# Sketch attention feeding an ELU MLP: the first two query groups computed from squares of sketch sums and differences

## The chip, the core and the metric

The kernel runs on one core of a Trainium2 chip. The metric is the device time of one execution in microseconds (us). The core has five engines with queues of their own: TensorE (PE in the profile; its weight loads are PEld), VectorE (DVE), ScalarE (ACT), GpSimd (POOL) and SyncE (SP, which only issues DMAs here). Each queue runs in program order; engines wait for one another through semaphores.

## The reference

```python
def phi(x):
    a = np.einsum('rd,bhsd->bhsr', S1, x)
    b = np.einsum('rd,bhsd->bhsr', S2, x)
    return np.einsum('bhsi,bhsj->bhsij', a, b).reshape(*x.shape[:-1], r * r)
q_p, k_p = (phi(q), phi(k))
kv = np.einsum('bhsf,bhsd->bhfd', k_p, v)
z = np.sum(k_p, axis=2)
num = np.einsum('bhsf,bhfd->bhsd', q_p, kv)
den = np.einsum('bhsf,bhf->bhs', q_p, z)[..., None] + 1e-06
attn = num / den
...
h = x @ w_in                                    # x: attn as (tokens, heads * 32)
g = np.where(h > 0.0, h, np.exp(np.minimum(h, 0.0)) - 1.0)
out = g @ w_out
```

There are 4 batches, 4 heads, 1088 positions, head size 32 and r = 8 sketches, so 64 features; 4352 tokens of 128 channels enter the MLP, whose hidden size is 2048. Everything is computed in float32. S1, S2, w_in and w_out arrive as float64 and are rounded to float32 on the chip.

## The kernel before, in words

The 4352 tokens are cut into groups of 512 (8 half tiles of 64 positions; the last group is smaller). Groups 0 and 1 belong to batch 0. For each group the attention part makes xg[g], a 128x512 tile with channels on partitions. The MLP then goes through 8 pairs of hidden chunks: mm1(g, cp) multiplies with w_in (L840, through the helper `quarters`, L253 to L257, which splits the 128 output columns into tiles of width[0] = 32), elu_a makes a relu and an exp on ScalarE (L861, L863), elu_d combines them on VectorE into gg (L869), and mm2 or its variants multiply with w_out. `steps` (L1004) gives the order of the pairs; mm2 runs two steps behind mm1. Everything is emitted by hand in the order that the queues are to have (`manual_schedule`), and the `extra` table hangs the attention work of later groups onto steps.

Rounding a weight chunk i is a chain: RA (VectorE, L102), RB (ScalarE, L107), then RS, RM, RD, RE on VectorE (L117, L121, L129, L137). Chunk 0 is w_in of pair 0, chunk 1 w_in of pair 1, chunk 2 w_out of pair 0, chunk 3 w_out of pair 1. RC_2 does RS, RM and RD of chunks 0 and 1 in one 512-wide instruction each.

Before the first mm1 the kernel must get batch 0's kv and z and the query features of group 0. The order, L946 to L1000:

- keep_warm (L260) issues matmuls of constants whose result nobody reads. L300 and L287 turn the sketch matrices into the tiles Sab, SXh and SW; `transp` (L280) turns k and q on VectorE.
- KF (L343) makes the key sketches, copied by ScalarE (L351). z_tile (L424), Z (L256) and Z_out (L465) make z. KO_pool (GpSimd, L322, tiles 0 to 3) and KO_first (VectorE, L416, tiles 4 to 8) make the 64 key features; KA (L435) sums kv over the positions. KS_first copies kv twice side by side (L481), turns it (L482) and stores it as kvS (L483).
- Group 0: q1_first (L505) makes the query sketches, copied by L509; q1z_first (L517) makes their products with z. q2_den multiplies and sums to den (L588, L593), takes the reciprocal (L594) and scales one sketch by it (L596); q2_out forms the 64 features per token and head as an outer product on VectorE (L609, two parts). q4_early turns them (L621, eight 128x128 turns on TensorE, each four copied by L622); q5_early multiplies with kvS (L628) and ScalarE copies the result to xg (L634).
- Group 1 goes the same way through q1_second (L526, L530), q2 and q4_early, interleaved with mm1_first and the first ELUs of group 0.

mm1_first (L847) is mm1 of group 0 and pair 0 in two column halves, outer loop over the halves. PSUM has eight banks, handed out by tag: "h" four in rotation, "aux" two, "o0" and "o1" one each. mm1 of a step writes to the "h" banks that the step two before used.

Of the kernel before, what the change touches and what calls it, by code (L numbers as in the profile page):

```python
# [27 lines left out]
def kernel(  # L28
# [21 lines left out]
    nc = tc.nc  # L50
# [45 lines left out]
    nc.gpsimd.memset(tiny[:], 2.0 ** -20)  # L96

# [206 lines left out]
    nc.gpsimd.tensor_copy(SW[:, :, :2, :].rearrange("p h x r -> p h (x r)"), Sab[:])  # L304

# [27 lines left out]
    kv_ps, feats, wzs, kf_ps = {}, {}, {}, []  # L333
# [106 lines left out]

    def KT_out(b):

        kt = work.tile([P, 2 * D], F32, name="kvt", tag="kvt")
        nc.vector.transpose(kt[:], kv_ps[b][:, :R * R])
        nc.sync.dma_start(kvd[b], kt[:])
        src = kvd[b].rearrange("(h p) x -> p h x", h=H)
        for w in range(4 if b in kvs else 0):
            nc.sync.dma_start(kvs[b][32 * w:32 * w + 32].rearrange("p h f d -> p h (f d)"), src)
        for u in (0, 1) if b in pair_b else (b // 2,):
            for f in range(2):  # L450
                r = slice(64 * u + 32 * f, 64 * u + 32 * f + 32)
                nc.sync.dma_start(kv2[b][r], src[:, :, D * f:D * f + D])
# [20 lines left out]
    def Z_first():  # L473
# [3 lines left out]
        return ps, ZC(0, ps)  # L477

    def KS_first():
        kd = work.tile([P, 2, R * R], F32, name="kd", tag="kd", bufs=1)  # L480
        nc.scalar.copy(kd[:], _ap(kv_ps[0][:, :R * R], [[0, 2], [1, R * R]]))  # L481
        nc.tensor.transpose(kv_ps[0][:, 128:256], kd[:].rearrange("p w f -> p (w f)"), ident[:])  # L482
        nc.scalar.copy(kvS[:].rearrange("p h d -> p (h d)"), kv_ps[0][:, 128:256])  # L483
# [16 lines left out]
    def q1_first():  # L500
        p = psum.tile([P, 512], F32, name="abqp", tag="aux")
        for i in range(4):
            for u in range(2):
                b, t = half_tile(0, 2 * i + u)
                nc.tensor.matmul(p[64 * u:64 * u + 64, i * 64:i * 64 + 64], qT[b][:, t, :],  # L505
                                 Sab[:].rearrange("p h y -> p (h y)"),
                                 skip_group_check=True, tile_position=(0, 64 * u))
        abw[0] = work.tile([P, H * 4, 2 * R], F32, name="abq", tag="abq", bufs=1)
        nc.scalar.copy(abw[0][:].rearrange("p (h t) y -> p h t y", h=H),  # L509
                       p[:, :256].rearrange("p (t h y) -> p h t y", t=4, h=H))  # L510

    def q1z_first():
        p = psum.tile([P, 512], F32, name="zqp", tag="h", bufs=4)
        for i in range(4):
            for u in range(2):
                b, t = half_tile(0, 2 * i + u)
                nc.tensor.matmul(p[64 * u:64 * u + 64, i * 32:i * 32 + 32].rearrange("p (h r) -> p h r", h=H),  # L517
                                 qT[b][:, t, :], SW[:, :, 2, :], skip_group_check=True, tile_position=(0, 64 * u))
        return p[:, :128].rearrange("p (t h r) -> p h t r", t=4, h=H)

    def q1_second():
        p = psum.tile([P, 512], F32, name="abwp", tag="h", bufs=4)
        for i in range(4):
            for u in range(2):
                b, t = half_tile(1, 2 * i + u)
                nc.tensor.matmul(p[64 * u:64 * u + 64, i * 96:i * 96 + 96], qT[b][:, t, :],  # L526
                                 SW[:].rearrange("p h x r -> p (h x r)"), skip_group_check=True,
                                 tile_position=(0, 64 * u))
        abw[1] = work.tile([P, H * 4, 3 * R], F32, name="abw1", tag="abq1", bufs=1)
        nc.scalar.copy(abw[1][:].rearrange("p (h t) y -> p h t y", h=H),  # L530
                       p[:, :384].rearrange("p (t h y) -> p h t y", t=4, h=H))


# [43 lines left out]
    def q2(g, parts=1, between=None):  # L577
        q2_den(g, None, between)
        q2_out(g, parts)

# [17 lines left out]

    def q2_out(g, parts=1, between=None):
        m = H * qn[g]  # L600
        x, an = abw.pop(g), ans.pop(g)
        qp[g] = work.tile([P, 4 * H, R, R], F32, name="qp", tag="qp", bufs=2)
        for i in range(parts):
            if i and between:
                between()
            h = slice(i * m // parts, (i + 1) * m // parts)
            a_ = an[:, h]
            b_ = x[:, h, :R]
            nc.vector.tensor_mul(qp[g][:, h], _ap(a_, list(a_.ap[1:]) + [[0, R]]),  # L609
                                 _ap(b_, [b_.ap[1], [0, R], b_.ap[2]]))  # L610

    def q4_early(g):

        qpT[g] = work.tile([P, H, 2, P], F32, name="qpT", tag="qpT", bufs=2)
        for hh in range(2):
            p = psum.tile([P, 512], F32, name="qtp", tag="aux")
            for h2 in range(2):
                for m in range(2):
                    o = (h2 * 2 + m) * P
                    r = (2 * hh + h2) * 4 + 2 * m  # L620
                    nc.tensor.transpose(p[:, o:o + P], qp[g][:, r:r + 2].rearrange("p t i j -> p (t i j)"), ident[:])  # L621
            nc.scalar.copy(qpT[g][:, 2 * hh:2 * hh + 2], p[:].rearrange("p (h m s) -> p h m s", h=2, m=2))  # L622

    def q5_early(g):
        xp = [psum.tile([P, 512], F32, name="xps", tag="aux") for _ in range(2)]
        for h in range(H):
            for w in range(2):
                nc.tensor.matmul(xp[w][D * h:D * h + D, :256], kvS[64 * w:64 * w + 64, h, :],  # L628
                                 qpT[g][64 * w:64 * w + 64, h].rearrange("p m s -> p (m s)"),
                                 skip_group_check=True, tile_position=(64 * w, D * h))  # L630
        xg[g] = work.tile([P, 512], F32, name="xg", tag="xg", bufs=3)
        to = xg[g][:].rearrange("p (m w s) -> p w m s", w=2, s=P)
        for w in range(2):
            nc.scalar.copy(to[:, w], xp[w][:, :256].rearrange("p (m s) -> p m s", s=P))  # L634

# [211 lines left out]
    def mm1_first():  # L847
        hs[0, 0] = [psum.tile([P, 512], F32, name="h", tag="h", bufs=4) for c in range(2)]
        for w in range(2):
            for c in range(2):  # L850
                cols = [x[:].rearrange("p (m w s) -> p w m s", w=2, s=P)[:, w] for x in (hs[0, 0][c], xg[0])]
                quarters(cols[0], W[:, 0, c * P:c * P + P], cols[1])
# [97 lines left out]
    zps, zl = Z_first()  # L950
    q1_first()
    KO_pool()
    KO_first(4, 5)
    KO_first(5, 7)
    Z(0, zps, zl)
    Z_out(0, zps)
    KO_first(7, KT)
    keep_warm(1, 96, 64)
    zq = q1z_first()
    q2_den(0, zq, lambda: RA(0))  # L960
    q2_out(0, 2, lambda: RA(1))
# [12 lines left out]
    keep_warm(1, 192, width[0])  # L974
    mm1_first()
    q2(1, 2, lambda: RA(2))
# [227 lines left out]
```

## Time and profile before

| what | value |
|---|---|
| median of 3 runs | 261.85 us (261.8 to 262.11) |
| the profiled execution's own time | 262.34 us |
| its span, first to last instruction | 260.6 us |
| mean granted TensorE clock | 0.998 |
| PE busy | 254.8 us (98%), 4123 matmuls |
| DVE busy | 186.9 us (72%), 352 instructions |
| ACT busy | 183.4 us (70%), 358 instructions |
| POOL busy | 159.0 us (61%) |

The span leaves out 1.74 us around the first and last instruction. Times in the trace count from the span's start. A line of the chain that ended last gives start, length, engine, the tile written, the source line and the number of instructions; a fp32 matmul call makes two TensorE instructions, a turn (transpose) makes one. A line of instruction groups gives line, engine, operation, output and input tiles, shape, count, then busy us and mean ns of one, then the idle time before them and what ended it. Busy shares are averages over stages with different limits; the stage in question here is the first 24 us.

### The profile page before, as it was taken

To read this page: it belongs to the slowest core of one execution; us is meant where nothing else is said; L and a number is where in the kernel's file an instruction comes from. 1 tells how busy PE (TensorE), PEld (TensorE's weight loads), DVE (VectorE), ACT (ScalarE), POOL (GpSimd) and SP (SyncE) were. 2 spreads that over 40 slices of the span, in tenths; PEclk is the share of its full clock that TensorE was granted. 3 is DMA by queue.
4 is the path that set the end of the run, shared out by engine and by line. 5 is a ranking of instruction groups with operands and counts; after the bars stand their busy time and mean duration, and the time that the engine had idled before them with its cause. 6 is when DMAs were issued, how large, how long until landed. Compare 5 with 4: busy or idle time off the path is not lost.

```text
span 260.6 us, 9756 instructions
## 1 busy us (share of the span) xinstructions
PE 254.8 (98%) x4123; PEld 158.4 (61%) x4123; DVE 186.9 (72%) x352; ACT 183.4 (70%) x358; POOL 159.0 (61%) x202
## 2 busy tenths in 40 slices
PE   8899999999999999999999999999999999999994
PEld 6753333453346667666666666665666666668993
DVE  6799999999988967997477675744466746544651
ACT  2379968766667577776687777775877777777792
POOL 3520007002179996788678798888688888887310
PEclk9999999999999999999999999999999999999999
DMA  5998079012112210002100204220001110110021
GB/s 173 330 358 222 3 223 268 24 21 85 28 18 28 31 34 18 3 15 34 20 0 4 33 10 104 60 30 13 3 3 27 34 26 3 25 19 3 3 30 33
DMA packets 30379, 15.61 MB, mean 60 GB/s; under 512 B 22496, under 2 KB 28000, under 8 KB 30336
## 3 DMA queue, kind: packets, MB, share of 16 engines
q1 hardware_dynamic: 29904, 14.63, 23.0%
q8 instruction: 32, 0.52, 0.9%
q10 hardware_dynamic: 368, 0.30, 0.3%
q0 software_dynamic: 64, 0.07, 0.1%
q14 instruction: 11, 0.09, 0.1%
HBM read 11.31 MB, written 2.36 MB: 52 GB/s over the span
## 4 chain that ended last, share of the span: by engine, by line
PE 97%; DVE 1%; ACT 0%; issue 0%; DVEq 0%
PE h L256 45%; PE pb L790 17%; PE pa L790 13%; PE o L256 5%; PE pb L766 4%; PE ol L256 3%; PE idle L264 1%; PE kv L435 1%; PE abp L343 1%; PE h L681 1%; PE h L551 1%; PE qtp L621 1%; DVE qp L609 1%; PE h L693 1%; PE xps L628 0%; PE kfps L365 0%
## 5 line engine op out<-in xcount | busy, mean ns | idle before, releaser
L256 PE MATMUL h<-xg,W 128*32 128x512 f32 (+3 forms) x904 | 130.8, 539 | 0.4 <-ACT xg L634 0.4
L869 DVE SCALAR_TENSOR_TENSOR gg<-e,h 128x512 f32<-128x512 f32 x128 | 85.9, 681 | 52.6 <-ACT e L863 47.8
L861 ACT ACTIVATE e<-h 128x512 f32<-128x512 f32 x128 | 75.5, 590 | 46.2 <-PE h L256 46.0
L863 ACT ACTIVATE e<-e 128x512 f32<-128x512 f32 x128 | 80.9, 632 | 3.8
L751 POOL TENSOR_TENSOR tt<-gg 128x512 f32<-128x512 f32 x50 | 64.3, 1286 | 28.9 <-DVE gg L869 25.2
L256 PEld LDWEIGHTS h<-xg,W 128*32 128x32 f32 (+1 forms) x904 | 43.0, 122 | 43.0 <-issue 34.4
L754 POOL TENSOR_TENSOR tt<-gg,tt 128x256 f32<-128x256 f32 x50 | 36.9, 739 | 3.9
L753 POOL TENSOR_TENSOR tt<-tt,gg 128x256 f32<-128x256 f32 x50 | 36.7, 734 | 3.9
L790 PEld LDWEIGHTS pa<-gg,W 128*64 128x64 f32 (+1 forms) x496 | 23.7, 126 | 22.4 <-issue 22.2
L790 PE MATMUL pa<-gg,W 128*64 128x128 f32 (+1 forms) x496 | 30.6, 274 | 0.0
L790 PE MATMUL pb<-tt,SS 128*64 128x128 f32 (+1 forms) x480 | 29.6, 273 | 0.0
L790 PEld LDWEIGHTS pb<-tt,SS 128*64 128x64 f32 (+1 forms) x480 | 22.8, 126 | 0.0
L790 PE MATMUL pa<-tt,SS 128*32 128x128 f32 (+1 forms) x288 | 21.2, 273 | 0.0
L790 PE MATMUL pb<-gg,SS 128*64 128x128 f32 (+1 forms) x256 | 19.9, 273 | 0.0
L790 PE MATMUL pb<-tt,W 128*64 128x128 f32 (+1 forms) x256 | 19.9, 273 | 0.0
L134 POOL TENSOR_TENSOR raw<-raw,tiny 128x512 f32<-128x512 f32 x1 | 1.0, 1041 | 24.7 <-DVE raw L129 24.7
L256 PE MATMUL o<-gg,W 128*32 128x512 f32 x128 | 15.3, 595 | 0.0
L790 PEld LDWEIGHTS pa<-tt,SS 128*32 128x32 f32 (+1 forms) x288 | 13.7, 124 | 0.0
L790 PEld LDWEIGHTS pb<-gg,SS 128*64 128x64 f32 (+1 forms) x256 | 12.8, 125 | 0.0
L790 PEld LDWEIGHTS pb<-tt,W 128*64 128x64 f32 (+1 forms) x256 | 12.8, 125 | 0.0
L766 PE MATMUL pb<-gg,W 128*32 128x256 f32 x192 | 11.5, 380 | 0.0
L921 DVE SCALAR_TENSOR_TENSOR gg<-e,h 128x256 f32<-128x256 f32 x16 | 6.6, 418 | 6.4 <-PE h L256 3.2
(163 smaller groups left out, 269.3 us busy)
## 6 DMA issues: line engine op xcount, KB each, us to landing
raw<-in_moe_w_in_dram SPq DMA_DIRECT2D x8, 256.0 KB, 6.3
raw<-in_moe_w_out_dram SPq DMA_DIRECT2D x8, 256.0 KB, 6.5
out_dram<-ob SPq DMA_DIRECT2D x112, 16.0 KB, 1.5
hd_k<-in_k_dram SPq DMA_DIRECT2D x3, 544.0 KB, 7.5
hd_q<-in_q_dram SPq DMA_DIRECT2D x3, 544.0 KB, 8.5
v<-in_v_dram SPq DMA_DIRECT2D x4, 288.0 KB, 7.1
v<-in_v_dram SPq DMA_DIRECT2D x4, 256.0 KB, 8.4
raw<-qpF SPq DMA_DIRECT2D x16, 64.0 KB, 2.0
```

The source lines that it names most:

```text
L256: nc.tensor.matmul(dst[c:c + tile], lhs[:, c:c + tile], rhs, skip_group_check=True, tile_position=(0, c), **kw)
L264: nc.tensor.matmul(idle[c:c + tile, :cols], ones[:, :tile], ones[:, :cols], skip_group_check=True, tile_position=(0, c))
L343: nc.tensor.matmul(ps[i // 5][64 * u:64 * u + 64, 64 * (i % 5):64 * (i % 5) + 64], kT[b][:, u * KT + i, :], Sab[:].rearrange("p h y -> p ( ...
L751: nc.gpsimd.tensor_tensor(_ap(t[:, 0], [[4 * P, 2], [P, 2], [1, P]]), _ap(gs[g, cp][:, 0, P:], [[4 * P, 2]] + us), _ap(gs[g, cp][:, 0], [[ ...
L753: nc.gpsimd.tensor_tensor(t[:, 1], t[:, 2], b11, op=ADD)
L754: nc.gpsimd.tensor_tensor(t[:, 3], b21, t[:, 1], op=SUB)
L766: nc.tensor.matmul(acc[1][0][r:r + width[0], 256 * hi:256 * hi + 256], lhs[:, w:w + width[0]], gg[:, c, 256 * u:256 * u + 256], start=(cp ...
L790: nc.tensor.matmul(bank[r:r + width[0], P * col:P * col + P], lhs[:, w:w + width[0]], rhs[:, u], start=(first and i in ((0,) if g == 1 els ...
L861: nc.scalar.activation(e, hs[g, cp][c][:, :n], RELU, scale=-1.0)
L863: nc.scalar.activation(e, e, EXP, scale=-1.0)
L869: nc.vector.scalar_tensor_tensor(gs[g, cp][:, c, :n], es[g, cp][:, c, :n], -1.0, hs[g, cp][c][:, :n], op0=ADD, op1=MAX)
L921: nc.vector.scalar_tensor_tensor(gs["last", k // 2][:, k % 2, :2 * P], es["last", k // 2][:, k % 2, :2 * P], -1.0, hs["last", k][:, :2 * P ...
```

## The change

Groups 0 and 1 no longer form the outer product of the two sketches a and b. Since a b = ((a + b)^2 - (a - b)^2) / 4, the change builds the 64 sums and 64 differences of sketch rows once (make_Spm) and lets one matmul per head (q_sums: 32 rows of one head, 128 output features, 512 tokens) produce all a + b and a - b with features on partitions. ScalarE squares them (q_squares, eight of 128x512). Because the features are already on partitions, no features are turned: x_sums multiplies the squares with kvS over all 128 rows, and KS_copy scales kvS's two halves by +0.25 and -0.25.

The division moves behind that sum. az makes, with 128 tokens as the stationary operand, one sketch and its product with z side by side; az_copy moves the first to SBUF, den_a and den_b make 1/den; den_wide (ScalarE) repeats each 1/den over its head's 32 channels; den_out turns that as four whole 128x128 blocks; den_copy brings it to SBUF; x_out multiplies it on VectorE with the x_sums result into xg.

In the order of the program, q_sums(0) stands where q1_first stood; the kv sum is split in two (KA_first: tiles 4 to 6 ahead of az(0), the rest after it); the second part of q is turned on VectorE before the first den; RC_2 is no longer used, chunks 0, 1 and 2 go through RS to RE one by one; the keep_warm calls behind the start are gone; mm1_first has the hidden chunk as its outer loop; width[0] is 64 from mm1_first to the first w_out, then 32 again. KT_out of batch 0 reads the SBUF copy kds of kv and no longer its PSUM bank.

```diff
+    quarters_pm = const.tile([P, 1], F32, name="qpm")
+    nc.gpsimd.memset(quarters_pm[:64], 0.25)
+    nc.gpsimd.memset(quarters_pm[64:], -0.25)
...
+    Sc = const.tile([FD, R], F32, name="Sc")
+    nc.scalar.copy(Sc[:], sps[:, :R])
...
+    Spm = const.tile([FD, 2, R, R], F32, name="Spm")
...
+    def make_Spm():
+        for s, op in enumerate((ADD, SUB)):
+            nc.vector.tensor_tensor(Spm[:, s], _ap(sps[:, R:], [[1, R], [0, R]]), _ap(Sc[:], [[0, R], [1, R]]), op=op)
...
+    def KA_first(tiles, first):
+        if first:
+            kv_ps[0] = psum.tile([P, 512], F32, name="kv", tag="o1", bufs=1)
+        for i in tiles:
+            for h in range(H):
+                nc.tensor.matmul(kv_ps[0][32 * h:32 * h + 32, :R * R], vt[0][:, (h * KT + i) * D:(h * KT + i + 1) * D],
+                                 feats[0, i // 5][:, i % 5, h].rearrange("p i j -> p (i j)"),
+                                 start=(first and i == tiles[0]), stop=(not first and i == tiles[-1]),
+                                 skip_group_check=True, tile_position=(0, 32 * h))
...
-        nc.vector.transpose(kt[:], kv_ps[b][:, :R * R])
+        nc.vector.transpose(kt[:], kv_ps[b][:, :R * R] if b else kds[0][:, 0])
...
-        return ps, ZC(0, ps)
-    def KS_first():
-        kd = work.tile([P, 2, R * R], F32, name="kd", tag="kd", bufs=1)
+        return ps
...
+    def KS_kd():
+        kd = kds[0] = work.tile([P, 2, R * R], F32, name="kd", tag="kd", bufs=1)
         nc.scalar.copy(kd[:], _ap(kv_ps[0][:, :R * R], [[0, 2], [1, R * R]]))
-        nc.tensor.transpose(kv_ps[0][:, 128:256], kd[:].rearrange("p w f -> p (w f)"), ident[:])
-        nc.scalar.copy(kvS[:].rearrange("p h d -> p (h d)"), kv_ps[0][:, 128:256])
+    def KS_turn():
+        nc.tensor.transpose(kv_ps[0][:, 128:256], kds[0][:].rearrange("p w f -> p (w f)"), ident[:])
...
+    def KS_copy():
+        nc.scalar.mul(kvS[:].rearrange("p h d -> p (h d)"), kv_ps[0][:, 128:256], quarters_pm[:])
...
-    def q1_first():
...
+    def tokens(g, rows, t0=0, t1=8):
+        b, t = half_tile(g, t0)
+        return qT[b][rows, t:t + t1 - t0, :].rearrange("p t s -> p (t s)")
...
+    def q_sums(g, half=None):
+        c = slice(0, 512) if half is None else slice(256 * half, 256 * half + 256)
+        for h in range(H):
+            if not half:
+                tag = "o0" if h == 3 else "h" if g or h == 2 else "aux"
+                sums[g, h] = psum.tile([P, 512], F32, name="qs", tag=tag, bufs={"o0": 1, "h": 4, "aux": 2}[tag])
+            rows = slice(32 * h, 32 * h + 32)
+            nc.tensor.matmul(sums[g, h][:, c], Spm[rows].rearrange("p s i j -> p (s i j)"),
+                             tokens(g, rows, c.start // 64, c.stop // 64), skip_group_check=True, tile_position=(32 * h, 0))
+
+    def q_squares(g, h):
+        if h % 2 == 0:
+            sq[g, h // 2] = work.tile([P, 2, 512], F32, name="sq", tag=("qp", "qpT")[g], bufs=2)
+        nc.scalar.square(sq[g, h // 2][:, h % 2], sums.pop((g, h))[:])
...
+    def az(g, p=None):
+        if p is None:
+            p = psum.tile([P, 512], F32, name="azp", tag="h", bufs=4)
         for i in range(4):
...
-    def q1z_first():
...
-    def q1_second():
...
+            nc.tensor.matmul(p[:, 128 + i * 64:192 + i * 64].rearrange("p (h y) -> p h y", h=H),
+                             tokens(g, slice(0, P), 2 * i, 2 * i + 2), SW[:, :, 1:, :].rearrange("p h x r -> p h (x r)"),
+                             skip_group_check=True)
+        dens[g] = p[:, 128:384].rearrange("p (t h x r) -> p h t x r", t=4, h=H, x=2)
...
+    def az_copy(g):
+        abw[g] = work.tile([P, H, 4, R], F32, name="aq", tag=f"aq{g}", bufs=1)
+        nc.scalar.copy(abw[g][:], dens[g][:, :, :, 0, :])
...
+    def den_a(g):
+        pw = pws[g % 2]
+        nc.vector.tensor_mul(pw[:, :4 * H, :R].rearrange("p (h t) r -> p h t r", h=H), abw.pop(g)[:], dens[g][:, :, :, 1, :])
...
+    def den_b(g):
+        pw = pws[g % 2]
+        den = dens[g] = work.tile([P, 4 * H], F32, name="dn", tag="den", bufs=2)
+        nc.vector.tensor_reduce(den[:], pw[:, :4 * H], axis=AX, op=ADD)
+        nc.vector.reciprocal(den[:], den[:])
...
+    def den_wide(g):
+        if not rb_all:
+            rb_all[0] = work.tile([P, 2, 512], F32, name="rbc", tag="kp", bufs=3)
+            rb_all[1] = work.tile([P, 4, P], F32, name="dx", tag="xg", bufs=3)
+        nc.scalar.copy(rb_all[1][:].rearrange("p t (h d) -> p t h d", h=H), _ap(dens[g][:], [[1, 4], [4, H], [0, D]]))
...
+    def den_out(g, **kw):
+        ps = rbs[g] = psum.tile([P, 512], F32, name="rb", **kw)
+        for t in range(4):
+            nc.tensor.transpose(ps[:, P * t:P * t + P], rb_all[1][:, t], ident[:])
...
+    def den_copy(g):
+        nc.scalar.copy(rb_all[0][:, g], rbs.pop(g)[:])
...
+    def x_sums(g, parts, half, **kw):
+        if half == 0:
+            xp[g] = psum.tile([P, 512], F32, name="xps", **kw)
+        c = slice(512 // parts * half, 512 // parts * (half + 1))
+        for h in range(H):
+            nc.tensor.matmul(xp[g][D * h:D * h + D, c], kvS[:, h, :], sq[g, h // 2][:, h % 2, c],
+                             skip_group_check=True, tile_position=(0, D * h))
...
+    def x_out(g, parts, half):
+        if half == 0:
+            xg[g] = work.tile([P, 512], F32, name="xg", tag="xg", bufs=3)
+        c = slice(512 // parts * half, 512 // parts * (half + 1))
+        nc.vector.tensor_mul(xg[g][:, c], xp[g][:, c], rb_all[0][:, g, c])
...
-    def q2(g, parts=1, between=None):
-        q2_den(g, None, between)
-        q2_out(g, parts)
...
-    def q2_out(g, parts=1, between=None):
...
-    def q4_early(g):
...
-    def q5_early(g):
...
     def mm1_first():
         hs[0, 0] = [psum.tile([P, 512], F32, name="h", tag="h", bufs=4) for c in range(2)]
-        for w in range(2):
-            for c in range(2):
-                cols = [x[:].rearrange("p (m w s) -> p w m s", w=2, s=P)[:, w] for x in (hs[0, 0][c], xg[0])]
-                quarters(cols[0], W[:, 0, c * P:c * P + P], cols[1])
+        for c in range(2):
+            for w in range(2):
+                quarters(hs[0, 0][c][:, 256 * w:256 * w + 256], W[:, 0, c * P:c * P + P], xg[0][:, 256 * w:256 * w + 256])
...
     transp(qT, "q", 0, 0, 8)
-    zps, zl = Z_first()
-    q1_first()
+    make_Spm()
+    zps = Z_first()
+    zl = ZC(0, zps)
+    q_sums(0)
     KO_pool()
     KO_first(4, 5)
     KO_first(5, 7)
+    KO_first(7, KT)
     Z(0, zps, zl)
+    KA_first((4, 5, 6), True)
     Z_out(0, zps)
-    KO_first(7, KT)
-    keep_warm(1, 96, 64)
-    zq = q1z_first()
-    q2_den(0, zq, lambda: RA(0))
-    q2_out(0, 2, lambda: RA(1))
-    KA(0)
-    KS_first()
-    keep_warm(1)
+    q_squares(0, 0)
+    q_squares(0, 1)
+    az(0, zps)
+    KA_first((0, 1, 2, 3, 7, 8), False)
+    RA(0)
+    az_copy(0)
+    q_squares(0, 2)
+    transp(qT, "q", 0, 8, NT)
     RB(0)
+    den_a(0)
+    den_b(0)
+    KS_kd()
+    q_squares(0, 3)
+    az(1)
+    KS_turn()
+    den_wide(0)
+    RA(1)
+    RS(0)
+    az_copy(1)
+    den_out(0, tag="aux", bufs=2)
+    KS_copy()
+    den_a(1)
+    den_b(1)
+    for f in (RM, RD, RE):
+        f(0)
+    den_copy(0)
+    x_sums(0, 2, 0, tag="aux", bufs=2)
+    x_sums(0, 2, 1)
+    den_wide(1)
+    q_sums(1)
+    den_out(1, tag="o1", bufs=1)
     RB(1)
-    q4_early(0)
-    transp(qT, "q", 0, 8, NT)
-    RC_2()
-    RE(0)
-    RE(1)
-    q1_second()
-    q5_early(0)
-    keep_warm(1, 192, width[0])
+    for h in range(H):
+        q_squares(1, h)
+    x_out(0, 2, 0)
+    x_out(0, 2, 1)
+    width[0] = 64
     mm1_first()
-    q2(1, 2, lambda: RA(2))
+    RA(2)
     RB(2)
-    elu_a(0, 0, 0)
-    elu_a(0, 0, 1, (0,))
-    mm1(0, 1, (0,))
-    q4_early(1)
+    for f in (RS, RM, RD, RE):
+        f(1)
+    RA(3)
+    for f in (RS, RM, RD, RE):
+        f(2)
+    elu_a(0, 0, 0, (0,))
+    den_copy(1)
+    elu_a(0, 0, 0, (1,))
+    elu_a(0, 0, 1)
+    x_sums(1, 1, 0, tag="aux", bufs=2)
+    mm1(0, 1)
     elu_d(0, 0, 0)
-    mm1(0, 1, (1,))
-    elu_a(0, 0, 1, (1,))
-    RC(2)
-    RA(3)
-    elu_a(0, 1, 0, (0,))
+    x_out(1, 1, 0)
     RB(3)
-    q5_early(1)
     elu_d(0, 0, 1)
     mm2(0, 0, True, False)
-    RA(4)
+    width[0] = 32
     for f in (RS, RM, RD):
         f(3)
-    elu_a(0, 1, 0, (1,))
+    RA(4)
+    elu_a(0, 1, 0)
     elu_a(0, 1, 1)
     RB(4)
     elu_d(0, 1, 0)
```

More of the change, by code (lines that the diff above doesn't have):

```diff
@@ L332 @@
     kvd = {b: dram.tile([P, 2 * D], F32, name=f"kvd{b}")[:] for b in range(B)}
-    kv_ps, feats, wzs, kf_ps = {}, {}, {}, []
+    kv_ps, feats, wzs, kds, kf_ps = {}, {}, {}, {}, []
     def KF(b):
@@ L497, in half_tile @@
         return (g // 2, 8 * (g % 2) + k) if g < NQ - 1 else (k, NT - 1)
-    def q1_first():
-        p = psum.tile([P, 512], F32, name="abqp", tag="aux")
-        for i in range(4):
[L503 to L510, printed above, removed]
@@ L512, in q1z_first @@
-    def q1z_first():
[L513 to L519, printed above, removed]
-    def q1_second():
[L522 to L531, printed above, removed]
+    sums, sq, dens, rbs, xp = {}, {}, {}, {}, {}
@@ new lines @@
+    rb_all = {}
+    def tokens(g, rows, t0=0, t1=8):
[10 more added lines that the diff above has]
+                             tokens(g, rows, c.start // 64, c.stop // 64), skip_group_check=True, tile_position=(32 * h, 0))
@@ L597, in q2_den @@
         ans[g] = an
-    def q2_out(g, parts=1, between=None):
[L600 to L610, printed above, removed]
-    def q4_early(g):
[L614 to L622, printed above, removed]
-    def q5_early(g):
-        xp = [psum.tile([P, 512], F32, name="xps", tag="aux") for _ in range(2)]
-        for h in range(H):
-            for w in range(2):
[L628 to L634, printed above, removed]
     exch = [raw_2[:, c].bitcast(F32).rearrange("p (e m a) w -> p e m (a w)", e=2, a=16) if wide else
@@ L848, in mm1_first @@
         hs[0, 0] = [psum.tile([P, 512], F32, name="h", tag="h", bufs=4) for c in range(2)]
-        for w in range(2):
-            for c in range(2):
-                cols = [x[:].rearrange("p (m w s) -> p w m s", w=2, s=P)[:, w] for x in (hs[0, 0][c], xg[0])]
-                quarters(cols[0], W[:, 0, c * P:c * P + P], cols[1])
+        for c in range(2):
+            for w in range(2):
+                quarters(hs[0, 0][c][:, 256 * w:256 * w + 256], W[:, 0, c * P:c * P + P], xg[0][:, 256 * w:256 * w + 256])
     def elu_a(g, cp, c, parts=(0, 1)):
```

## The prediction, as put on record before the result

> **What bounds the kernel now.** I read the chain that ended last first, in order of time over the first 45 us; each line gives start, length and the work.
>
> ```profile
> 8.50 0.61 PE abqp L505 x16
> ...
> 13.34 0.63 PE qtp L621 x4
> 13.96 0.85 PE abwp L526 x16
> 14.81 0.70 PE xps L628 x16
> 15.52 0.64 ACT xg L634 x2
> 16.15 0.10 issue
> 16.25 2.79 PE h L256 x40
> 19.04 1.02 PE qtp L621 x8
> 20.07 0.99 PE h L256 x8
> 21.06 0.59 PE xps L628 x16
> 21.65 1.85 PE o L256 x16
> 23.51 3.43 PE h L256 x32
> ```
>
> From 16.25 us on the chain lies on TensorE alone, and it stays there to the end (PE has 97% of the chain). Before that it passes from engine to engine. So the span is the moment at which TensorE enters its gapless stream plus a fixed amount of matmul work. The timeline puts the first w_out matmul at 21.58 and the mm1 that follows it (group 1, pair 0) at 23.32. The change ends there; **its effect is how far that 23.32 moves**, if the other engines keep up afterwards. The busy time by stretch says how much room they have.
>
> ```profile
> 8.43:21.58 13.15, 11.98 (x243) 7.23 (x235) 11.98 (x31) 8.28 (x19) 4.15 (x10) 1.00 1.09 340
> ```
>
> The columns behind the length are PE, weight loads, VectorE, ScalarE, GpSimd, granted clock and DMA. In the stretch that is rewritten TensorE and VectorE are busy 11.98 of 13.15 us, ScalarE only 8.28.
>
> **The rules of the walk.** I laid the instructions on their queues in program order with durations from rows. Two xg copies of 0.38 took 0.65 together, so independent ScalarE neighbours overlap by 0.11; two qp products of 0.69 took 1.29, so on VectorE I take 0.08; a dependent neighbour starts 0.03 after the end. Between engines I take 0.06, and 0.13 more behind a matmul. A 512-column mm1 group streams at 0.86 (1.72 for two), a 256-column one at 0.43. A change of TensorE's tile shape costs 0.06. That last term is fitted: the old order, walked with it, gives 16.30, 21.59 and 23.32 where the trace has 16.25, 21.58 and 23.32.
>
> **The change, part by part.** TensorE first. From 8.43 to the first w_out the old order has 11.35 us of matmuls by this walk, 1.03 of it the keep_warm fillers. The new one has 11.68: two q_sums at 0.95, Z 0.15, the kv sums 1.22, two az at 1.00, the kv turn 0.15, two den_out of four turns at 0.55, x_sums 0.86 and 0.86, mm1_first 1.72, mm1 1.72. So **the instructions get fewer but their time does not fall**; what can be won is only the old order's gaps, and 11 changes of tile shape (0.66) remain.
>
> Two of these terms have no row. az is a full 128x128 weight load for 64 columns: eight loads at the 0.106 of qtp's loads are 0.86 at least; sps (L300), two such matmuls in 0.50, would make it 2.00. I take eight qtp spacings of 0.128, hence 1.00, since qtp has the same shape of load at the same clock. q_sums is eight matmuls of 512 columns, one head per 32-row strip. If four strips run at once it is two passes of 0.43, 0.86; if none overlap, 3.44. The nearest row is L551, 32x32 tiles in all 16 places:
>
> ```profile
> 60.00 0.40 PE L551 MATMUL h<-qT,SWs 32*32 32x256 f32 x2
> ...
> 60.65 1.93 PE L256 MATMUL o<-gg,W 128*32 128x512 f32 x16
> ```
>
> Thirty-two matmuls of 256 columns, 0.21 each, passed in 0.65 instead of 6.8, so row strips overlap here. I take 0.86 plus about 0.09 for one exposed 128-column weight load, 0.95. The Trainium skill ("TensorE: Matmul & The Clock Gate", Part 3, measured speedup) gives four row strips at 512 columns 3.07 times, not 4; by it q_sums would be 1.12 and the sum below +0.40 instead of +0.06. No 32x128 tile is in this trace to decide.
>
> ScalarE. These rows price its part:
>
> ```profile
> L861 ACT ACTIVATE e<-h 128x512 f32<-128x512 f32 x4 | 2.4, 594 | 0.4 <-PE h L256 0.4
> L622 ACT COPY qpT<-qtp 128x512 f32<-128x512 f32 x4 | 2.2, 588 | 0.4 <-PE qtp L621 0.3
> L107 ACT ACTIVATE W<-W,ebias 128x256 uint32<-128x256 uint32 x4 | 1.9, 506 | 0.7 <-DVE W L102 0.7
> L634 ACT COPY xg<-xps 128x256 f32<-128x256 f32 x4 | 1.3, 370 | 0.2 <-PE xps L628 0.2
> ```
>
> It loses four qpT copies, four xg copies, abq and abw: 2.35 + 1.48 + 0.37 + 0.48 = 4.7. It gains eight squares of 128x512 from PSUM (no row; bounds 0.55 and the 0.63 of the exp, taken 0.59 as relu and copy), two az copies of 0.27, two den_wide (0.63, read from SBUF as the exp is; down to 0.55) and two den_copy of 0.59: 7.7. That is 3.0 more, 11.3 of 13.15; the free 4.9 covers it only where the order lets it.
>
> VectorE loses four qp products (0.69) and two an (0.29), and gains x_out (two of 0.425, priced by the 128x256 kp product, and 0.69), make_Spm and the splitting of RC_2 into two of 0.41, 0.30 and 0.44. make_Spm (two of 0.225, as Sab) falls into the 0.74 idle before the first kp product. If that cover went, kp and all behind it would be 0.3 late. The second q transpose moves from 13.11 to 10.24; the last packets of its load end at 9.70, and the issue order of SP's queue is unchanged. GpSimd gets two memsets before 1 us, ahead of its identity; VectorE waits for the sketches until 2.49 anyway.
>
> **The path that sets 23.32.** q_sums(0) starts where abqp did, 8.57 in the walk, +0.95; Z and the first kv sums with their changes, az(0) at 10.27, done 11.27. az copy 11.39 to 11.66; den_a, reduce, reciprocal (0.29, 0.30, 0.25) to 12.62. den_wide is queued on ScalarE behind square 4, which ends at 13.07: it runs to 13.70. den_out 13.76, x_sums 14.37 to 15.23, q_sums(1) 15.29 to 16.24. Its four squares, 0.48 apart, 16.43 to 18.35; RB(2) behind them to 18.86, for which VectorE waits 0.35. Then RS, RM, RD, RE of w_out to 20.50, the first gg 0.60, x_out(1) 0.61, the second gg 21.71 to 22.39; the second half of w_out 22.45 to 23.32, and a change of shape: **23.38, against 23.32**. TensorE alone would have the first w_out at 21.33 (8.57 + 11.68 + 0.66 + 0.42 of waiting for den_wide), 0.25 ahead, and then it waits 0.26 for that second gg. In other words, the gaps at 11.8 and 16.2 go, and VectorE and ScalarE become late instead. x_out(0) ends 16.66, so mm1_first starts at 16.91, TensorE's own queue, not 16.25; its c-outer order and the missing turns give that back.
>
> Behind it nothing new binds: walked to pair 4, TensorE stays gapless; the tightest place, mm1 of (0,3), has gg 0.9 before it. So +0.06 for the profiled execution, 262.34 + 0.06 = 262.40 (span 260.6 + 0.06, with the same 1.74 around it). That execution lies 0.49 above the median, so I predict **261.9**.
>
> **The rivals.** About 0.2% (0.52 us) is what can be told from no change.
> 1. Forecast, within 0.52 either way: **0.42**.
> 2. Faster. The unpriced terms fall to their low ends: q_sums 0.86, az 0.86, squares, den_wide and den_copy 0.55. The walk gives 22.74, -0.58, hence 261.3. q_sums counts twice on the path, the square five times. For it: the weight loads are pulled ahead everywhere else in the trace. Against: it needs nearly all terms at once. With the walk's own error, **0.28**.
> 3. Slower: the 32-row strips overlap only in pairs (1.75 each). Place: both q_sums stand on the path, so the price is twice the excess: 2 x 0.80 + 0.06 = 1.66, hence 263.5. It decides from 1.18 per q_sums. Against it speaks L551. **0.14**.
> 4. Slower: ScalarE binds. It runs without a gap from 16.4 to 24 in the walk; a square of 0.70 costs 0.72, 262.6, and from 0.67 it decides. **0.10**.
> 5. Slower: Square and exp call for different activation tables. One load is 1.28 (L155). The load ahead of the first square falls into waiting, the one ahead of the first elu exp delays the gg: +1.24, 263.1. The Trainium skill ("ScalarE: Activation LUTs", Table sets) names relu, copy, identity and abs as being in every set, not square; the trace has one load for exp, relu and copy and shows no square. **0.06**.
>
> The three slower ones make 0.30. The fillers' removal I give nothing: the longest TensorE gap left in the walk is 0.42, and the granted clock is 1.00 through gaps of 0.39 now. The range takes in 2 in part and 3 to 5 up to 263.3, and goes down to 260.9 for an early error of the walk.
>
> **What would show it.** q_sums: TensorE's next instruction about 0.95 after the first of eight. az likewise 1.0. Squares 0.48 apart. The first w_out near 21.3 with its second half waiting for gg, and the next mm1 at 23.4. A gap of TensorE before q_sums(1) or a second table load would make the prediction wrong, and so would any wait after 24 us.

## The result and the profile after

The changed kernel takes 262.64 us (median of 20 runs, 261.92 to 267.32), the kernel before beside it 261.99 (20 runs, 261.77 to 262.61). The ratio is 1.0026 [1.0016, 1.0036]: **slower by about 0.65 us**, in the forecast's range (260.9 to 263.3), just above the 0.2% that the forecast of 261.9 called no change. Two slow runs, both with a granted clock of 0.981, are left out of the ratios, spans and counts: one of the changed kernel (267.32 us) and one of its form with the second part of q first (268.75 us).

The profiled execution of the changed kernel took 262.32 us, its span is 260.5. This is the chain that ended last, as start, length and work, from 8 us to the mm1 behind w_out.

```profile
8.33 1.07 PE qs L541 x8
9.40 0.24 PE zps L259 x4
9.64 0.47 PE kv L458 x24
10.11 1.07 PE zps L553 x8
...
11.20 0.27 ACT aq L560
11.47 0.50 ACT sq L547
11.97 0.39 ACT W L110
...
12.52 0.50 ACT sq L547
13.02 0.51 ACT dx L577
...
13.58 0.66 PE rb L582 x4
14.24 1.00 PE xps L592 x16
15.24 1.07 PE qs L541 x8
16.31 0.59 PE rb L582 x4
16.89 1.88 PE h L259 x16
18.77 0.99 PE xps L592 x8
19.77 1.87 PE h L259 x8
21.64 1.83 PE o L259 x8
```

Up to q_sums(1) it is the path of the forecast: q_sums(0) (qs L541), Z, the first kv sums, az(0) (zps L553), the az copy, squares and den_wide (dx) on ScalarE, den_out (rb), x_sums, q_sums(1). From there the forecast went over the squares, RB(2), VectorE and the second gg; the chain stays on TensorE, which has no gap from 13.58. The timeline has the first w_out at 21.47 (forecast 21.33), the mm1 behind it at 23.39 (forecast 23.38). So these two executions meet the walk's last number, and their spans are as good as equal, 260.6 and 260.5; the last part shows that the first of these agreements is luck. Busy times by stretch, columns as before:

```profile
8.43:21.58 13.15, 12.70 (x167) 6.96 (x169) 10.47 (x30) 10.77 (x25) 2.93 (x10) 1.00 1.08 335
```

TensorE is busy 12.70 of 13.15 us with 167 instructions in place of 11.98 with 243; the work moved from VectorE (11.98 to 10.47) to ScalarE (8.28 to 10.77). Fewer instructions, more time on TensorE. From 8 to 24 us TensorE waits for one thing, 0.5 us for den_wide.

**A gap remains.** Two equal spans do not give 0.65 us. Taking each run's time less its span shows where it sits; in the means of these runs 0.46 us of the loss lie outside the span and 0.28 inside:

| runs | median us | span, median (range) | time less span, median (range) |
|---|---|---|---|
| before (28 runs of one comparison) | 261.93 | 260.15 (260.0 to 260.5) | 1.77 (1.73 to 1.83) |
| changed (the 19 runs above) | 262.64 | 260.5 (260.1 to 261.3) | 2.39 (1.76 to 2.79) |

Outside the span the kernel before always spends the same; the changed one spends over 2.0 in 12 of 19 runs. The profiled execution was one of those that did not (1.82). And inside the span the medians are 0.35 apart: the profiled execution of before was a late one (260.6 where its median is 260.15).

### The profile page after: what moved, and what is told of

It is laid out like the page before. It is cut to its first block, busy times and chain, and to the rows that moved or that the text cites. A ratio compares the mean times of both kernels' runs of the same rounds, so it can differ in the third digit from the quotient of the medians.

```text
span 260.5 us, 9608 instructions
## 1 busy us (share of the span) xinstructions
PE 255.5 (98%) x4045; PEld 158.1 (61%) x4045; DVE 185.8 (71%) x354; ACT 185.7 (71%) x363; POOL 158.2 (61%) x204
## 3 DMA queue, kind: packets, MB, share of 16 engines
HBM read 11.31 MB, written 2.36 MB: 52 GB/s over the span
## 4 chain that ended last, share of the span: by engine, by line
PE 97%; ACT 1%; issue 0%
PE h L259 45%; PE pb L815 17%; PE pa L815 13%; PE o L259 5%; PE pb L791 4%; PE ol L259 3%; PE idle L267 1%; PE kv L447 1%; PE abp L355 1%; PE qs L541 1%; PE h L706 1%; PE xps L592 1%; PE h L618 1%; PE h L718 1%; PE kfps L377 0%; PE rb L582 0%
## 5 line engine op out<-in xcount | busy, mean ns | idle before, releaser
L259 PE MATMUL o<-gg,W 128*32 128x512 f32 (+1 forms) x120 | 15.4, 595 | 0.0
```

The costliest lines, as they stand in the source:

```text
L259: nc.tensor.matmul(dst[c:c + tile], lhs[:, c:c + tile], rhs, skip_group_check=True, tile_position=(0, c), **kw)
```

## The experiments

**Theory F**: outside the span, the execution's end waits for a fetch of TensorE's own instructions. The trace has a queue of kind "instruction" (q8) with packets of 16 KB. In the kernel before there are 32 of them, one for every 250 traced instructions of TensorE on the mean (31 steps from the 375th to the 8113th). TensorE has 8307 traced instructions before the change and 8149 after it, and the last packet's place relative to the program's end moved with that. **Theory W**: inside the span, the loss is the walk's own terms, mis-sized. Rivals: D, the order of the loads, since the moved turn of q waits for its load; GpSimd's added memsets at the start; and later G, that padding helps by moving the early fetches.

**Both kernels again**, unchanged, on one chip.

> The kernel before, unchanged, for the span of each of its runs (so far only its times are known). Theory D (the moved q transpose waits for its load, whose landing varies from run to run): its spans lie within 0.3 us of one another, since the old order reaches that transpose at 13.1, 3 us after the load; time minus span is as large and as scattered as in the changed kernel. Rival O (the added time lies outside the span): time minus span stays at 1.7 to 2.0 here, where the changed kernel has 1.8 in some runs and 2.4 to 2.8 in others.

> The changed kernel, unchanged, beside the kernel before on the same chip. Theory D: median 0.3 to 0.9 us above the kernel before, spans scattered over about 1 us upward from 260.1. Rival O: median 0.3 to 0.9 us above, spans no longer than those of the kernel before (median within 0.2), time minus span larger by about 0.5.

Measured: before 261.86 (ratio 0.9996 [0.9988, 1.0005]), spans 260.0 to 260.2, time less span 1.73 to 1.83. Changed: 262.73 (1.0024 [1.0015, 1.0034]), spans 260.1 to 260.7 (median 260.4, 0.25 above before), time less span over 2.0 in 7 of 9 runs (median 2.50). Most of the added time lies outside the span, as O says; D, which expected the same scatter in the kernel before, is out as the main cause. The profiled execution of the latter (span 260.4, time less span 2.25) shows what comes after its last instruction. Its line for the instruction queue in the DMA view of 260.6 to 266 us gives packets, MB and share:

```profile
q8 instruction: 1, 0.02, 1.5%
```

One packet, of the instruction queue, in flight from 261.63 to 262.89 us. The same view of before, of its repeat and of the first profiled execution of the changed kernel has no packet; there the last fetch came at 251.4, 251.0 and 256.1. Of the later runs one more profiled execution has a large time less span, 2.96, that of the kernel with the second part of q first (below). It too has one packet behind its last instruction, at 262.51, from 264.32 to 265.70 (view of 262.6 to 268 us):

```profile
q8 instruction: 1, 0.02, 1.6%
```

Counted from the start of the span, the time of each of these two executions ends 0.24 us before the packet has landed: a late packet and a long time go together by the same distance. None of the other twelve profiled executions has a packet there, and their time less span is 1.73 to 1.89.

**The second part of q first.** Its load ahead of v and of the first w chunk on SP's queue, because the moved turn of q waits 0.49 us for it.

```diff
+    load_hd(nc.sync, "q", q, 0, 8, NT)   # ahead of v and w chunk 0
...
-    load_hd(nc.sync, "q", q, 0, 8, NT)
```

> The changed kernel with the load of the second part of q issued ahead of v and of the first weight chunk, so that it lands about 1.5 us earlier. Theory D: VectorE's wait for that load (0.49 us) is gone, the spans draw together at the low end, and the median falls by 0.4 to 0.7 to that of the kernel before. Rival O: the wait goes too, but the median stays within 0.2 us of a_again, because the time was never inside the span.

Measured: 264.39 (six runs; 1.009 [1.0057, 1.0124]), time less span up to 2.96 and over 2.0 in 4 of 6 runs. VectorE's wait for q is gone, as both expected, but v now lands at 11.31 and the kv sums wait 1.7 us for it, so neither forecast of the median came. An earlier second part of q at v's cost is no remedy.

**GpSimd's memsets later.** The two quarter scales set behind pw's, not ahead of the identity.

```diff
-    nc.gpsimd.memset(quarters_pm[:64], 0.25)     # and [64:], -0.25, at the start
...
+    nc.gpsimd.memset(quarters_pm[:64], 0.25)     # and [64:], -0.25, behind pw
```

> The changed kernel with the two new GpSimd memsets of the quarter scales moved from the start of GpSimd's queue behind the pw memsets, so that GpSimd starts as in the kernel before. Theory D: no change against a_again (within 0.2). Rival O, in the form that the longer start of GpSimd's queue adds the time ahead of the span: time minus span returns to 1.8 and the median falls by 0.4 to 0.6.

Measured: 262.74 (1.0028 [1.0019, 1.0036]), span 260.3, time less span up to 2.92 and over 2.0 in 8 of 11 runs. No effect. (Its profiled execution, with 1.75, shows no last fetch at all: 31 packets, the last at 248.6.)

**TensorE's program longer, at its start.** 78 and 30 more pairs of weight load and matmul in the warm-up, of the same length in time, so that every fetch comes earlier.

```diff
-    keep_warm(3)
-    keep_warm(1, 224)
+    keep_warm(3, 128)        # 30 pairs: keep_warm(3, 256)
+    keep_warm(10, 64, 32)    #           keep_warm(4, 64, 32)
```

> The changed kernel with 78 more TensorE load-and-matmul pairs in the idle warm-up before 4.4 us (more and narrower matmuls of constants in about the same time), so that TensorE's program is as long as that of the kernel before. Theory F: the added time is the end of the program waiting for TensorE's last 16 KB instruction fetch, whose trigger the shorter program has within its last 26 instructions, the old one 194 instructions before its end. F expects time minus span at 1.7 to 1.8 in every run, and a median 0.4 to 0.6 below a_again, that is 0.1 to 0.3 above the kernel before. Rival I (all of the loss lies in the first 24 us, in q_sums waiting for q's load): no change against a_again, time minus span scattered up to 2.8 as there.

> The same with 30 more pairs: the trigger then lies about 86 instructions, some 4 us, before the end of TensorE's program. Theory F: most runs at 1.7 to 1.8 between time and span, a few above, median 0.3 to 0.6 below a_again. Rival I: as a_again.

Measured: with 78 pairs time less span is 1.73 to 1.84 in all 11 runs, with 30 pairs 1.74 to 1.89 in all 12, as F says. The times are 262.64 (1.0034 [1.0018, 1.0051]) and 262.20 (1.0020 [1.0005, 1.0035]), so F's median came with 30 pairs and failed with 78. With 78 pairs the gain is lost again inside the span, median 260.8: the first 16 KB fetch moves from 13.3 us to 8.09, among the loads, and the chain now begins with a load:

```profile
4.60 7.10 DMA hd_q<-in_q_dram
...
11.73 0.78 DVE qT L283
```

The second part of q lands at 11.71, where the unpadded kernel turned it at 10.64.

**The same in the kernel before**, 50 pairs in the warm-up (keep_warm(1, 256) and keep_warm(7, 112, 32)), to put its last fetch where the changed kernel has it.

> The kernel before with 50 more such pairs in the warm-up, so that its program ends as the changed one's does, about 28 instructions behind a trigger of the fetch. Nothing else of the change is in it. Theory F: spans as in b_again, time minus span scattered from 1.7 to 2.8, median 0.3 to 0.6 above the kernel before. Rival I: no change (within 0.1).

Measured: 266.51 (1.0167 [1.015, 1.0184]), but time less span stays at 1.75 to 1.86. F's expectation failed. The added time (4.6 us in the median, 3.6 in the profiled execution) is in the span; 2.6 of the 3.6 are a hole in the middle of the kv sums, beside a first fetch from 11.01 to 12.16:

```profile
9.94 1.14 PE L435 MATMUL kv<-kp,v 128*32 128x64 f32 x65
...
13.64 0.32 PE L435 MATMUL kv<-kp,v 128*32 128x64 f32 x7 [2.56 <-issue]
```

TensorE stops for 2.56 us after 65 of 72 matmuls, waiting for nothing that the profile shows. That it had run out of fetched instructions is argued from the fetch beside it, not shown, and the hole lasts 1.5 us beyond that fetch. Padding at the start thus moves things in the load phase, so the last pads stand at the end.

**78 pairs, and make_Spm ahead of the first turn of q.**

```diff
+    make_Spm()
     transp(qT, "q", 0, 0, 8)
-    make_Spm()
```

> a_pad78 with make_Spm moved ahead of the first q transpose on VectorE, where VectorE waits 0.35 to 0.7 for q's first load in the profiles of the changed kernel. Theory F plus a late start of q_sums(0): q_sums(0) starts up to 0.25 earlier in runs where q lands late, the spans draw in to 260.0 to 260.4, median 0.1 to 0.2 below a_pad78. If q's load does not hold q_sums(0) back, no difference (within 0.1).

Measured: 262.66 (1.0024 [1.0015, 1.0033]), span 260.85: the same as 78 pairs alone. The expected gain did not come; in both profiled executions the chain waits for the second part of q, turned from 11.43 here, and not for the first.

**The program longer, at its end.** 40 and 4 small matmul calls on constants behind the last w_out, beside the last output's way to memory.

```diff
         if last[k - lag][1] == NP - 1:
             fin_last(last[k - lag][0])
+    idle = psum.tile([P, 512], F32, name="idle2", tag="h", bufs=4)
+    keep_warm(10, 64, 32)     # 4 calls: keep_warm(1, 64, 32); before: keep_warm(6, 64, 32)
```

> The changed kernel with 40 small matmul calls on constants (80 weight loads and 80 matmuls, 160 of TensorE's instructions) at the very end of TensorE's program, behind the last w_out, beside the last output's copy and DMA. Nothing moves in the load phase or in the chain. Theory F (the time that is lost outside the span is an instruction fetch that TensorE sets off only with its last few instructions, and that then lands after the last of them): the fetch comes while the tail still runs, time minus span is 1.72 to 1.89 in every run, the span stays at 260.2 to 260.6 as in the unchanged kernel, the median is 262.1 to 262.3, ratio about 1.001. Rival G (what the earlier padding changed was the timing of the fetches in the load phase, not the place of the last one): time minus span goes on scattering up to 2.9, median 262.6.

> As the one before, with 4 calls at the end (8 weight loads and 8 matmuls) instead of 40. Theory F: 16 more instructions move the trigger from 21 to 38 instructions before the end of the program to 37 to 54; if the threshold is close to the end, time minus span is 1.72 to 1.89 in most runs, median 262.1 to 262.4; if the fetch has to be some microseconds ahead of the end, it scatters as before, median 262.6. Rival G: it scatters, median 262.6.

> The kernel before with 24 calls at the end of TensorE's program (48 weight loads and 48 matmuls), which puts its last fetch as far from the end of the program (19 to 36 instructions) as it is in the changed kernel (21 to 38), with nothing moved in the load phase. Theory F, if the distance from the end is all that counts: time minus span scatters from 1.75 to 2.9, span 260.1, median 262.3 to 262.7, ratio 1.001 to 1.003. If what counts is how long TensorE still runs after the trigger, or rival G: time minus span 1.72 to 1.89, median 261.95, ratio 1.000.

Measured, changed kernel: 262.14 (1.0007 [0.9997, 1.0018]) with 40 calls and 262.15 (1.0010 [0.9998, 1.0023]) with 4; time less span 1.74 to 1.81 in all 11 runs and 1.73 to 1.94 in all 12. Against the kernel before beside them, that is 0.26 and 0.27 us where the unpadded kernel has 0.65 and 0.80. **With sixteen instructions whose result nobody reads, the loss is some 0.4 to 0.5 us smaller.** The intervals of the ratios overlap; it is the time less span that tells the kernels apart. Nothing early moved, which speaks against rival G. One rival was not tested: all runs with a longer program were made on another chip than the repeat of the unpadded kernel, and the unpadded kernel was not run on that chip. For F and against the chip speak the traces: the two packets behind the end, and the times that follow them.

Measured, kernel before with 24 calls: 263.08 (1.0048 [1.0036, 1.006]), 1.2 us slower for 0.9 us of matmuls that end at 257.4, nearly three microseconds before its usual last instruction. None of the expected outcomes came: the added time is in the span (261.1 to 261.6), with time less span 1.73 to 1.95. The DMA view of 250 to 266 us says how; first before's repeat, then this kernel:

```profile
q8 instruction: 1, 0.02, 0.4%
...
out_dram<-ol SPq DMA_DIRECT2D x1, 32.0 KB, 1.9
out_dram<-ol ACTq DMA_DIRECT2D x1, 32.0 KB, 2.1
```

```profile
q8 instruction: 2, 0.03, 0.8%
...
out_dram<-ol SPq DMA_DIRECT2D x1, 32.0 KB, 3.1
out_dram<-ol ACTq DMA_DIRECT2D x1, 32.0 KB, 3.2
```

There is one fetch more, from 258.01 to 258.97, and the last two output DMAs, under way at that moment, take 1.1 to 1.2 us longer from issue to landing. Other traces fit: with 30 pairs at the start a fetch from 253.94 to 255.45 meets the two outputs that GpSimd issues, which take 3.6 us in place of 1.9, off the end's path; and in the trace of before, the outputs of 16 KB issued about a fetch (from 1.6 us ahead of its start to 0.8 behind) have a median of 2.1 to 3.2 us beside seven of nine fetches, against 1.5 for all of them. So what the last fetch costs depends on what it meets: the outputs (inside the span) or nothing but the end itself (outside).

**The sketch sums of group 1 in halves**, the first one in TensorE's wait for den_wide, with the 40 calls at the end.

```diff
     az_copy(1)
+    q_sums(1, 0)
     den_out(0, tag="aux", bufs=2)
...
     den_wide(1)
-    q_sums(1)
+    q_sums(1, 1)
```

> The changed kernel with the 40 calls at the end, and the sketch sums of group 1 in two halves of 256 columns: the first half ahead of the turn of group 0's 1/den, in the 0.45 us that TensorE waits there, the second half where the whole was. A walk of the queues with the changed kernel's own durations gives 0.15 us less at the first matmul after w_out. Theory F together with that walk: time minus span 1.72 to 1.89, span 260.0 to 260.4, median 262.0, ratio 1.000 (0.999 to 1.001). Theory H (the loss inside the span is on VectorE, which starts group 0's products no sooner): the span stays at 260.4, median 262.2.

Measured: 262.0 (1.0005 [0.9997, 1.0013]), span 260.2. Theory W's side of it: the chain lies on TensorE alone, with no wait.

```profile
12.74 0.64 PE qs L541 x8
13.38 0.59 PE rb L582 x4
13.97 1.00 PE xps L592 x16
14.97 0.65 PE qs L541 x8
```

The halves cost 1.29 in place of 1.07, and the 0.45 of waiting is gone. The span is 0.2 below that of the 40 calls alone; the ranges overlap (259.8 to 260.9 and 260.2 to 260.8), but in the profiled executions the way from the first matmul of kv's sketch sums to the mm1 behind w_out is 15.42 in place of 15.70 (table below). So theory H (that VectorE holds the loss) falls. This is the best form of the change that was run, and it is level with the kernel before, not ahead of it.

## Why the forecast came out as it did

**Inside the span** the two profiled executions mislead, since before's began its stream late: its first matmul of kv's sketch sums (zps) is at 7.82, that of its repeat at 7.44. From that common point to the mm1 behind w_out, the executions compare like this (left out are those in which the second part of q, v or the hole sets the path):

| execution | first part of q turned from | zps | mm1 behind w_out | difference |
|---|---|---|---|---|
| before | 6.39 | 7.82 | 23.32 | 15.50 |
| before, again | 6.37 | 7.44 | 22.94 | 15.50 |
| before, 24 calls at the end | 7.10 | 7.58 | 23.09 | 15.51 |
| changed | 6.81 | 7.65 | 23.39 | 15.74 |
| changed, again | 7.14 | 7.26 | 23.24 | 15.98 |
| changed, memsets later | 6.49 | 7.34 | 23.22 | 15.88 |
| changed, 30 pairs at the start | 6.68 | 7.54 | 23.25 | 15.71 |
| changed, 40 calls at the end | 6.49 | 7.37 | 23.07 | 15.70 |
| changed, 4 calls at the end | 7.42 | 7.67 | 23.76 | 16.09 |
| halves | 6.39 | 7.25 | 22.67 | 15.42 |

The forecast's difference was 23.38 - 7.82 = 15.56, that is +0.06. Measured is +0.20 to +0.24 in three executions whose first part of q came in time, +0.38 in a fourth (0.11 of it ahead of az(0), for a reason that was not traced), and +0.48 and +0.59 where that part came late. That the walk's 23.38 met 23.39 was luck: the execution that it started from was 0.38 later than its repeat, the changed one 0.17 earlier at zps, and the walk 0.18 too short. Counted from zps (7.82 for the forecast, 7.65 in the first profiled execution of the changed kernel), the moments are:

| moment | forecast | measured |
|---|---|---|
| q_sums(0) begins | 0.75 | 0.61 |
| az(0) begins | 2.45 | 2.44 |
| den_out begins | 5.94 | 5.93 |
| q_sums(1) begins | 7.47 | 7.52 |
| mm1_first begins | 9.09 | 9.17 |
| first w_out | 13.51 | 13.82 |
| mm1 behind w_out | 15.56 | 15.74 |

Point by point:

- **q_sums**, 0.95 each: mis-sized. TensorE's next instruction comes 1.07 after the first of eight. The walk adds 0.06 for the change of tile shape behind it, so each is 0.12 above the bare term and 0.06 above what the walk gives it with that change. 3.44 for the eight without overlap, over 1.07, is 3.2 times, not 4. The Trainium skill ("TensorE: Matmul & The Clock Gate", Part 3, measured speedup) gives 3.07 times, hence an estimate of 1.12; the trace is nearer to that than to my 0.95. The excess of the first q_sums does not reach az(0), since the walk has q_sums(0) itself begin 0.14 too late (8.57, where the trace of before has the matmuls in its place at 8.43).
- **az**, 1.00: right. From the first of az(0) to its copy it takes 1.11, in the walk 1.12 (1.00 and what is added behind a matmul).
- **mm1_first, x_sums(1), mm1** are the larger part of the 0.31 by which the first w_out comes late: 1.88 to the next piece against 1.78 in the walk, 1.00 against 0.92, 1.77 against 1.72, together 0.23. The 0.08 ahead of them is x_sums(0), 1.00 against 0.92, and q_sums(1), less some small gains.
- **The wait for the second gg**: 0.06 in place of 0.26. The second half of w_out begins 0.49 behind the matmul before it, which a 512-column matmul group without a wait does in 0.43, and 0.05 after that gg ends. VectorE's path is 0.11 late there, TensorE's own queue 0.31; so about 0.20 of the lateness comes back, and the second half of w_out itself adds 0.08 (1.01 to the mm1 behind it, 0.93 in the walk).
- **Squares, den_wide, den_copy**: 0.60, 0.63 and 0.60 alone, forecast 0.59, 0.63 and 0.59; group 1's squares begin 0.48 to 0.49 apart, forecast 0.48. Right. TensorE's wait for den_wide: 0.45, forecast 0.42.
- **A second table load** (rival 5): there is one load in the trace, as before. Square ran beside exp without its own. **ScalarE binding** (rival 4) did not come, though its 262.6 is the time that was measured: the squares took 0.60, not 0.67 or more. **Strips in pairs** (rival 3) did not come. The low-end terms (rival 2) did not either.
- **No wait after 24 us**: right. TensorE has none.
- **The moved turn of q**, counted as nothing: it waits about 0.5 for its load in every execution of the changed kernel in this table but one (0.23 with 30 pairs), which the chain hardly feels (the den behind it starts at 11.51, the az copy ends at 11.47). What the walk left out is that the first part of q can land late. The prediction names the place: "If that cover went, kp and all behind it would be 0.3 late." make_Spm now stands on VectorE between the turn of q's first part and the key products (kp), and both q_sums(0) and the first kv sums need what comes of it. In the repeat (turned from 7.14) the chain starts at that load and goes over make_Spm to q_sums(0); with 4 calls at the end (turned from 7.42) it goes over make_Spm and kp to the kv sums, and the difference grows to 16.09. First the repeat, then that one:

```profile
1.98 5.14 DMA hd_q<-in_q_dram
...
7.14 0.71 DVE qT L283
7.86 0.25 DVE Spm L316 x2
```

```profile
7.42 0.71 DVE qT L283
8.13 0.24 DVE Spm L316 x2
8.37 1.54 DVE kp L428 x3
...
10.00 0.54 PE kv L458 x24
```

The kernel before does not feel it: turned from 7.10, its difference is 15.51. This fits the changed kernel's spans, which reach up to 261.3 where before's rarely leave 260.0 to 260.5; the execution turned from 7.42 has a span of 261.2.

**Outside the span** is where a step failed: "with the same 1.74 around it". In the kernel before it is 1.72 to 1.84; in the changed one it is larger where the last fetch of TensorE's instructions comes behind the last instruction. The runs of the changed kernel without a longer program (its first comparison, its repeat, the second part of q first, the later memsets) have 31 of 45 over 2.0; those with one have none of 68. With the tail the kernel is 0.26 above before (262.14 against 261.88; the interval of the ratio takes in 1), without it 0.65 and 0.80: about 0.4 to 0.5 us of the loss go with the fetch, the other 0.26 or so lie in the span. The Trainium skill ("Runtime: NRT & Kernel Launch", Instruction fetch mechanics) has the instructions refilled in blocks of 16 KiB, which are 256 instructions, at a cost "mostly hidden". The packets here agree with the size of the block, and one for every 250 traced instructions with the count; at the end of the program the cost is not hidden here.

What stays open: from which instruction the fetch is set off, and why it comes in time in some executions and not in others of the same kernel. In the unpadded changed kernel 8128 of 8149 traced instructions had begun when the last one came in time, all of them when it came late, and in one execution with 1.75 it does not show at all. With 4 calls at the end 29 instructions were left, in the kernel before with 50 pairs 34, without a loss at the end. The distance alone does not tell when it costs.

So none of the rivals came, and the likeliest case, within 0.52 us of the kernel before, was missed by 0.13 (0.65). The range held because it was wide. The walked part is off by about 0.2 through TensorE's terms, q_sums and the matmuls from mm1_first on, and by more where q lands late; the rest is a cost that the walk did not hold at all, of a program that ends at another place in its last block of instructions.

## What to carry over

Subtract the span from each run's time before explaining a change of less than 1%: what grows there has nothing to do with the chain. A change in the number of instructions shifts every instruction fetch, in the load phase and at the end; a few idle matmuls behind the last real one are a cheap test, though in one kernel here they cost 1.2 us. And compare two executions from a common point on the chain, not from the span's start, since a profile can begin its stream 0.4 us late.

## What the runs showed of the hardware

- An instruction fetch of 16 KB takes 0.9 to 1.6 us in these traces. Beside the last outputs they landed 1.1 to 1.2 us later; beside the input loads it came with a load 1.1 us later; behind the last instruction it went with an execution up to 1.2 us longer (time less span 2.96 against 1.8).
- Four 32-row strips with 128 columns of weights and 512 of data: eight fp32 matmuls in 1.07 us; the same work in halves of 256, 1.29.
- Square on ScalarE ran beside exp, relu and copy with the one table load that the kernel before has, 0.60 for 128x512 from PSUM.
